# Routing's products over two slots and two banks, stores issued by ScalarE, and a later weight split, in a three-stage FFN kernel on one core

## The chip, the cores and the metric

The kernel runs on one core of a Trainium2 chip. The metric is the device time of that core in microseconds (us), the median of several executions. The engines are TensorE (PE; PEld is its weight load, which overlaps with the products), VectorE (DVE), ScalarE (ACT), GpSimd (POOL) and SyncE (SP), which in this kernel issues nearly all DMAs.

## The reference

Three computations follow each other, all in fp32, over 3072 tokens (4 batches of 768) of 256 numbers.

```python
# 1: attention with a decaying state, in chunks: x (4,8,768,32), a, B, C (state 16)
M = (C @ B^T) * L            # L: products of a, causal
y = M @ x + (C @ state) * decay_to_i ; state = decay_full * state + sum(B x decay_from_j)
# 2: FFN with a leaky unit, 256 -> 2048 -> 256
h = x @ w_in
g = np.maximum(h, 0.0) + alpha * np.minimum(h, 0.0)
x = g @ w_out
# 3: eight experts, one per token, 256 -> 1024 -> 256
logits = x @ w_gate + modality_bias[modality_id]
e_idx = np.argmax(logits, axis=1)
...
out[mask] = gate_w[mask, None] * (np.maximum(x[mask] @ w1[e], 0.0) @ w2[e])
```

## The kernel before

**Stages.** The tokens are 24 chunks of 128, in nine blocks of 2, 2, 2 and then six times 3 chunks (block 0 to 8). A block goes through attention, the first FFN, and routing. The routed rows are scattered to a table `srt` in DRAM, sorted by expert. At the end there are 14 *items*, each a page of 256 sorted rows with the weights of one expert. Every large fp32 product is made of three, from operands split in a high and a low part (xh, xl; wi_h, wi_l; gh, gl).

**Slots.** From block 3 on the order of all work is written out by hand: a list of slots, 16 for each of the six late blocks (one for each 128 of the 2048 inner columns) and 8 for each item. A slot holds six products that make `ph` of its own column, ACT's `t` and VectorE's `g` from it, the split of the slot before (ACT's `gh`, POOL's `gl`), and six products `px` of the column four slots earlier. `do(u, fn, ...)` puts one more step at the end of slot u. Each engine runs what it has strictly in that order. `at[k, c]` is the slot of block k, column c; `ui` is the first slot of the items.

**Routing.** Block k is routed in the slots of block k+1 (u is the first of them). For each chunk t of the block, `route_mm` makes the product `pxr` of the FFN's result with an identity and the gate's weights, and one slot later `route_act` has VectorE add the logits `L` and ACT copy the rows to `xr`. `route_b` finds the best expert, `route_exp` and `route_gate` its probability, `route_c` ranks the rows (the product `pr`), `route_d` scatters them.

**Banks.** PSUM has three buffers for `ph` (routing of blocks 0 to 2 takes from these), the banks x0, x1 and x2 (`px`, and in x2 one `pxr`, `pr` or, for items, `pt` at a time), and two buffers `s` (`ps`, the attention scores, which VectorE's `mt` reads; and an item's second `px3`).

**The split of B and C.** In the late blocks B and C come from a DRAM tile `bcs` of three bf16 parts. They are made in two groups: chunks 13 to 20 in columns 1 to 6 of block 3, chunks 21 to 23 in columns 1 to 6 of block 5. Each step (`split_part`) has ACT cast a part to a tile `part` (three buffers), VectorE subtract it from `rbc`, and a DMA store the part. `load_chunk` reads `bcs` again, on SP: one load of `ab` and five of `bs` for each chunk.

**The items' start.** `item_split(i, ...)` splits an item's weights, in eight steps, one a slot: an ACT cast and a VectorE subtraction. `tail_counts` casts the counts to `cnti` and issues eight stores on SP which clear the rows behind each expert's last one (`srt<-zr`); the loads of item 2's weights (`raw`) follow them on SP. `table_at` places five small steps that work out which expert a page has.

Of the kernel before, what the change touches and what calls it, by code (L numbers as in the profile page):

```python
# [8 lines left out]
F32 = mybir.dt.float32  # L9
# [10 lines left out]
P = 128  # L20
NB, NH, SEQ, HD, DS = 4, 8, 768, 32, 16
# [91 lines left out]
def ssm_moe_moe_kernel(  # L113
# [21 lines left out]
    nc = tc.nc  # L135
# [13 lines left out]
    ps_s = ctx.enter_context(tc.tile_pool(name="ps_s", bufs=2, space=PS))  # L149


    def mm(o, l, r, start, stop):
        nc.tensor.matmul(o, l, r, start=start, stop=stop)  # L153
# [4 lines left out]
    def vsub(o, x, y):  # L158
        nc.vector.tensor_tensor(o, x, y, ALU.subtract)  # L159
# [8 lines left out]
    bcs = dram.tile([2, NCH, 3, DS, NH * P], BF16, name="bcs")  # L168
# [190 lines left out]
    m2p = []  # L359
# [104 lines left out]
                tc.declare_no_dep(d.ins, o, reason="rows are disjoint")  # L464
            tails.append(d.ins)

    def route_ps(k, shape, nm):
        if k < NS:
            return ps_h.tile(shape, F32, tag="h", name=nm)
        return ps_x.tile(shape, F32, tag="x2", name=nm)  # L470

    def route_a(k, ts=None):

        n = blocks[k][1]
        for t in range(n) if ts is None else ts:
            route_mm(k, t)
            route_act(k, t)

    def route_mm(k, t):
        if t == 0:  # L480
            blk[k]["xr"] = work.tile([P, MX, ROW], F32, tag="xr", name="xr", bufs=2)
            blk[k]["L"] = small.tile([P, MX, NE], F32, tag="L", name="L")
        p = route_ps(k, [P, 512], "pxr")
        ts_ = slice(t * P, (t + 1) * P)
        pk = p[:, :KD * (P + NE)].rearrange("p (k w) -> p k w", k=KD)
        for kk in range(KD):
            mm(pk[:, kk], blk[k]["xT"][:, kk, ts_], idwg[:, kk], True, True)
        blk[k]["pk"] = pk
# [45 lines left out]
    def route_c(k):  # L534
        c0, n = blocks[k]
        oh = blk[k]["oh"]
        pr = route_ps(k, [P, 5, NE], "pr")
        for t in range(n + 1):
            for u in range(t):
                mm(pr[:, t], one, oh[:, u], u == 0, t == n and u == n - 1)  # L540
            if t < n:
                mm(pr[:, t], tri, oh[:, t], t == 0, True)
        blk[k]["pr"] = pr
# [405 lines left out]
    last = len(blocks) - 1  # L949
    slots = [("m",) + q for q in late] + [("i", i, fc) for i in range(NSTATIC) for fc in range(KF2)]  # L950
    at = {q[1:]: u for u, q in reversed(list(enumerate(slots))) if q[0] == "m"}
    ui = len(late)
# [3 lines left out]
    def do(u, fn, *args):  # L956
        todo.setdefault(u, []).append((fn, args))
# [42 lines left out]
    def split_part(g, j, q):  # L1000
        c0 = NEXACT + g * 8
        n = min(8, NCH - c0)
        r = blk["r", g, j]
        t = parts[-1].tile([P, NH * P], BF16, tag="part", name="part", bufs=3)
        nc.scalar.copy(t[:n * DS], r[:n * DS])
        if q < 2:
            vsub(r[:n * DS], r[:n * DS], t[:n * DS])
        nc.sync.dma_start(bcs[j, c0:c0 + n, q], t[:n * DS])

    def tail_counts():  # L1010
        nc.vector.tensor_copy(cnti, cnt)
# [11 lines left out]
    def route_at(k, mms, b):  # L1023
        for t, u in enumerate(mms):
            do(u, route_mm, k, t)
            do(u + 1, route_act, k, t)
        for v, fn in zip(b, (route_b, route_exp, route_gate, route_c, route_d)):
            do(v, fn, k)

    u = at[NS, 0]  # L1030
    route_at(1, (u, u + 1), (u + 4, u + 5, u + 6, u + 5, u + 6))
    route_at(2, (u + 5, u + 6), (u + 9, u + 10, u + 11, u + 10, u + 14))
    for k in range(NS, last + 1):
        u = at[k, 15] + 1
        if k < last - 1:
            route_at(k, (u + 4, u + 5, u + 6), (u + 8, u + 9, u + 12, u + 10, u + 13))
        else:
            route_at(k, (u + 4, u + 5, u + 6), (u + 7, u + 8, u + 9, u + 8, u + 9))

    def table_at(u, j, pool):  # L1040
        steps = []

        def step():
            if not steps:
                steps.append(item_tables(j, pool[-1]))
            next(steps[0], None)

        for v in range(u, u + 5):
            do(v, step)

    table_at(at[last - 1, 14], 0, small_)
    table_at(at[last, 10], 1, m2p)
    do(at[last, 15], tail_counts)
    table_at(ui + 11, 2, m2p)

    for k in range(NS, last):
        c0, n = blocks[k + 1]
# [3 lines left out]
        for j in range(n):  # L1061
            c, b = c0 + j, at[k, 0] + 5 * j - (k > NS)
# [11 lines left out]
    for g, u, v in ((1, None, at[NS, 1]), (2, at[NS + 1, 8], at[NS + 2, 1])):  # L1074
        if u is not None:
            do(u, split_load, g)
        for q in range(6):
            do(v + q, split_part, g, q % 2, q // 2)
# [10 lines left out]
    do(ui + 3, item_tr_act, 1)  # L1089
    for q in range(8):  # L1090
        do(at[last, 6] + q, item_split, 0, q // 2, (q % 2,))
        do(at[last, 11] + q, item_split, 1, q // 2, (q % 2,))
    for i in range(2, NSTATIC):
        b = ui + KF2 * (i - 2)
        do(b, item_load, i, 1 if i >= NFULL else 2)
        do(b if i == 2 else b + 5, item_rows, i)
        b += KF2
        for q in range(8):
            do(b + q, item_split, i, q // 2, (q % 2,))
        do(b + 4, item_tr_mm, i)  # L1100
        do(b + 5, item_tr_act, i)
# [102 lines left out]
```

## Time and profile before

| | |
|---|---|
| median of 3 runs | 628.76 us (627.92 to 630.45) |
| profiled execution, its own time | 629.47 us |
| its span | 627.7 us |
| mean granted TensorE clock | 0.938 |
| PE busy | 559.2 us |
| DVE busy | 438.0 us |
| ACT busy | 318.6 us |
| POOL busy | 242.0 us |
| DMA | 92.15 MB, mean 147 GB/s |

The span reaches from the first to the last instruction of the profiled execution; some 1.8 us of its time lie outside. A matmul's busy time contains its overlap with the next one. The granted clock is a share of full speed: 1.00 is 2.4 GHz, 0.50 is 1.2 GHz.

### The profile page before, as it was taken

Reading aid. Unit: us, or ns where it says so; the run is one execution under the profiler, and the core shown is the slowest. Engines: PE = TensorE matmul, PEld = TensorE weight load, DVE = VectorE, ACT = ScalarE, POOL = GpSimd, SP = SyncE. Lnnn points to the kernel's source line nnn. Section 1 sums busy time; section 2 is a strip of 40 time slices with the busy share of each in tenths; the row PEclk is TensorE's granted clock in tenths of the full one; section 3 lists DMA queues with packets and bytes.
Section 4 is the critical chain, followed back from the end, with each engine's and each line's share of the span. In section 5 each row is a group of like instructions: output and inputs, shape, how many; then the busy total and the mean of one; then the engine's idle time right before and its main releaser. Section 6 shows DMA issues by size and latency. Waiting matters only on the chain. (4 is left out here: it accounts for less than half of the span.)

```text
span 627.7 us, 12104 instructions
## 1 busy us (share of the span) xinstructions
PE 559.2 (89%) x4271; PEld 522.6 (83%) x4271; DVE 438.0 (70%) x861; ACT 318.6 (51%) x702; POOL 242.0 (39%) x258
## 2 busy tenths in 40 slices
PE   8988778998969989949989989988778999999994
PEld 7866667898869878938979979978778999999994
DVE  4997879935857756846766757549729787787770
ACT  0463655655634443624444434455526776776761
POOL 1142444654534635824654834635203121122211
PEclk9786797999869999979999999999898999999998
DMA  7967664310234325214214210270597977677500
GB/s 236 296 216 240 196 185 158 129 45 9 82 92 151 119 76 162 86 55 130 101 69 131 93 68 2 85 243 26 162 280 256 353 221 233 221 227 228 178 24 7
DMA packets 60563, 92.15 MB, mean 147 GB/s; under 512 B 5102, under 2 KB 37040, under 8 KB 60496
## 3 DMA queue, kind: packets, MB, share of 16 engines
q1 hardware_dynamic: 58096, 84.99, 43.0%
q0 software_dynamic: 2400, 6.32, 2.7%
q8 instruction: 36, 0.59, 0.4%
q14 instruction: 31, 0.25, 0.1%
HBM read 75.59 MB, written 15.96 MB: 146 GB/s over the span
## 5 line engine op out<-in xcount | busy, mean ns | idle before, releaser
L616 POOL TENSOR_TENSOR gl<-g,gh 128x384 fp32r<-128x384 f32 (+1 forms) x144 | 145.5, 1014 | 170.7 <-ACT gh L614 168.2
L607 DVE SCALAR_TENSOR_TENSOR g<-ph,sal,t 128x384 f32<-128x384 f32 (+1 forms) x144 | 81.0, 565 | 91.5 <-ACT t L605 91.4
L605 ACT ACTIVATE t<-ph,sgn 128x384 f32<-128x384 f32 (+1 forms) x144 | 78.4, 545 | 129.7 <-PE ph L153 128.4
L153 PE MATMUL ph<-xh,wi_h 128*128 128x384 f32 (+1 forms) x288 | 100.9, 351 | 12.9 <-DVE g L607 12.7
L153 PE MATMUL px<-gh,wo_h 128*128 128x384 f32 (+1 forms) x288 | 95.7, 333 | 2.4 <-ACT wo_h L424 1.4
L153 PE MATMUL px<-gl,wo_h 128*128 128x384 f32 (+1 forms) x288 | 96.1, 334 | 1.5 <-POOL gl L616 1.5
L153 PE MATMUL px<-gh,wo_l 128*128 128x384 f32 (+1 forms) x288 | 95.0, 331 | 0.0
L153 PE MATMUL ph<-xl,wi_h 128*128 128x384 f32 (+1 forms) x288 | 94.3, 328 | 0.3 <-DVE xl L159 0.3
L153 PE MATMUL ph<-xh,wi_l 128*128 128x384 f32 (+1 forms) x288 | 94.2, 327 | 0.0
L614 ACT CAST gh<-g 128x384 fp32r<-128x384 f32 (+1 forms) x144 | 67.5, 469 | 20.9 <-DVE g L607 20.6
L875 POOL DMA_INDIRECT out_dram<-ob,xr x26 | 28.4, 1092 | 111.9 <-ACT ob L874 26.4
L153 PEld LDWEIGHTS ph<-xh,wi_h 128*128 128x128 f32 x288 | 56.7, 198 | 17.6 <-DVE g L607 14.5
L852 ACT ACTIVATE rh<-ph 128x256 fp32r<-128x256 f32 (+1 forms) x112 | 41.5, 371 | 55.4 <-PE ph L153 55.1
L853 DVE SCALAR_TENSOR_TENSOR rl<-ph,rh 128x256 fp32r<-128x256 f32 (+1 forms) x112 | 45.0, 402 | 27.0 <-ACT rh L852 26.0
L153 PEld LDWEIGHTS px<-gh,wo_h 128*128 128x128 f32 x288 | 57.8, 201 | 2.8 <-ACT wo_h L424 1.6
L153 PEld LDWEIGHTS px<-gl,wo_h 128*128 128x128 f32 x288 | 57.4, 199 | 3.2 <-POOL gl L616 2.2
L153 PEld LDWEIGHTS px<-gh,wo_l 128*128 128x128 f32 x288 | 57.7, 201 | 0.2 <-issue 0.2
L153 PEld LDWEIGHTS ph<-xl,wi_h 128*128 128x128 f32 x288 | 56.8, 197 | 0.8 <-DVE xl L159 0.8
L153 PEld LDWEIGHTS ph<-xh,wi_l 128*128 128x128 f32 x288 | 56.7, 197 | 0.0
L153 PE MATMUL ph<-x2h,wi_h 128*128 128x256 f32 x144 | 41.6, 289 | 2.8 <-DVE rl L853 2.8
L962 DVE TENSOR_TENSOR_SCAN ab<-ab,id 128x512 f32<-128x512 f32 x30 | 43.6, 1453 | 0.0
L567 POOL DMA_INDIRECT srt<-xr,pi x24 | 25.5, 1062 | 43.4 <-DMA raw<-in_w_dram 29.9
(149 smaller groups left out, 1312.7 us busy)
## 6 DMA issues: line engine op xcount, KB each, us to landing
raw<-in_w_dram SPq DMA_DIRECT2D x56, 512.0 KB
ab<-a_scr SPq DMA_DIRECT2D x24, 512.0 KB
srt<-zr SPq DMA_DIRECT2D x8, 645.0 KB
raw<-in_w_in_dram SPq DMA_DIRECT2D x8, 512.0 KB
raw<-in_w_out_dram SPq DMA_DIRECT2D x8, 512.0 KB
bs<-bcs SPq DMA_DIRECT2D x38, 96.0 KB
bs<-bcs SPq DMA_DIRECT2D x19, 192.0 KB
xr<-srt SPq DMA_DIRECT2D x14, 258.0 KB
```

The lines of the kernel that those rows point to most:

```text
L153: nc.tensor.matmul(o, l, r, start=start, stop=stop)
L567: sc = nc.gpsimd.indirect_dma_start(out=srt[:, :], out_offset=bass.IndirectOffsetOnAxis(ap=pi[:, t:t + 1].bitcast(U32), axis=0), in_=xr[:, ...
L605: nc.scalar.activation(t[:, :N], ph[:, :N], AF.Copy, scale=sg)
L607: nc.vector.scalar_tensor_tensor(g[:, :N], ph[:, :N], sal[:, fc:fc + 1], t[:, :N], ALU.mult, ALU.max)
L614: nc.scalar.copy(gh[:, :N], g[:, :N])
L616: nc.gpsimd.tensor_tensor(gl[:, :N], g[:, :N], f(gh[:, :N]), ALU.subtract)
L852: nc.scalar.activation(rh[:, :n], ph[:, :n], AF.Relu)
L853: nc.vector.scalar_tensor_tensor(rl[:, :n], ph[:, :n], 0.0, f(rh[:, :n]), ALU.max, ALU.subtract)
L875: nc.gpsimd.indirect_dma_start(out=out[:, :], out_offset=bass.IndirectOffsetOnAxis(ap=xr[:, t, ROW - 1:ROW].bitcast(U32), axis=0), in_=ob, ...
L962: nc.vector.tensor_tensor_scan(lt[:, s_].rearrange("p h i -> p (h i)"), lt[:, s_].rearrange("p h i -> p (h i)"), id8[:, s_].rearrange("p h ...
```

## The change

There are three edits.

First, the routing of blocks 3 to 8: the second chunk's product moves from one slot behind the first to two, the third's to three, and the third takes a buffer of `s` and no longer bank x2. Steps b to d of blocks 1, 2, 7 and 8 are put in other slots to suit; those of blocks 3 to 6 stay.

Second, the twelve stores in `split_part` are issued by ACT and not by SP.

Third, the split of item 1's weights starts four slots later, so that half of it lies in item 0's slots; the item tables, `tail_counts` and the loads of later items' rows move by one slot. Lines of the changed kernel are two higher from `route_ps` on.

```diff
-    def route_ps(k, shape, nm):
+    def route_ps(k, shape, nm, t=0):
         if k < NS:
             return ps_h.tile(shape, F32, tag="h", name=nm)
+        if t == 2:
+            return ps_s.tile(shape, F32, tag="s", name=nm)
         return ps_x.tile(shape, F32, tag="x2", name=nm)
...
-        p = route_ps(k, [P, 512], "pxr")
+        p = route_ps(k, [P, 512], "pxr", t)
...
-        nc.sync.dma_start(bcs[j, c0:c0 + n, q], t[:n * DS])
+        nc.scalar.dma_start(bcs[j, c0:c0 + n, q], t[:n * DS])
...
     u = at[NS, 0]
-    route_at(1, (u, u + 1), (u + 4, u + 5, u + 6, u + 5, u + 6))
-    route_at(2, (u + 5, u + 6), (u + 9, u + 10, u + 11, u + 10, u + 14))
+    route_at(1, (u, u + 1), (u + 4, u + 5, u + 6, u + 6, u + 8))
+    route_at(2, (u + 5, u + 7), (u + 9, u + 10, u + 11, u + 11, u + 14))
     for k in range(NS, last + 1):
         u = at[k, 15] + 1
         if k < last - 1:
-            route_at(k, (u + 4, u + 5, u + 6), (u + 8, u + 9, u + 12, u + 10, u + 13))
+            route_at(k, (u + 4, u + 6, u + 7), (u + 8, u + 9, u + 12, u + 10, u + 13))
         else:
-            route_at(k, (u + 4, u + 5, u + 6), (u + 7, u + 8, u + 9, u + 8, u + 9))
+            route_at(k, (u + 4, u + 6, u + 7), (u + 8, u + 9, u + 10, u + 10, u + 10))
...
-    table_at(at[last, 10], 1, m2p)
-    do(at[last, 15], tail_counts)
-    table_at(ui + 11, 2, m2p)
+    table_at(at[last, 11], 1, m2p)
+    do(ui, tail_counts)
+    table_at(ui + 12, 2, m2p)
...
-        do(at[last, 11] + q, item_split, 1, q // 2, (q % 2,))
+        do(at[last, 15] + q, item_split, 1, q // 2, (q % 2,))
...
-        do(b if i == 2 else b + 5, item_rows, i)
+        do(b if i == 2 else b + 6, item_rows, i)
```

**PE, a middle block's route.** In block 4's slots PE's rows from the first `pxr` of block 3 on read as follows before (the second `pxr` is the last row; between the two stand the scores `ps` and one slot's twelve products, of which four rows are shown).

```order
L153 MATMUL pxr<-idwg,xT 128x136 x2
...
L153 MATMUL ps<-bs 128x128
L153 MATMUL ph<-xh,wi_h 128x384
...
L153 MATMUL px<-gh,wo_l 128x384
L153 MATMUL px<-gl,wo_h 128x384
L153 MATMUL pxr<-idwg,xT 128x136 x2
```

After the change the row that follows those twelve products is the weight load of the next scores:

```order
L153 MATMUL px<-gh,wo_h 128x384
L153 MATMUL px<-gh,wo_l 128x384
L153 MATMUL px<-gl,wo_h 128x384
L153 LDWEIGHTS bs
L153 MATMUL ps<-bs 128x128
```

The second `pxr` has moved behind the next slot's twelve products, the third behind one slot more.

**ACT, columns 4 to 6 of block 5.** Here stand the last casts of the second group (48 partitions are three chunks) and the copies `xr` of block 4's route. Before:

```order
L325 CAST xh<-py 128x2x128
L1005 CAST part<-rbc 48x1024
L605 ACTIVATE t<-ph,sgn 128x384
L614 CAST gh<-g 128x384
L497 COPY xr<-pxr 128x256
L1005 CAST part<-rbc 48x1024
L605 ACTIVATE t<-ph,sgn 128x384
L614 CAST gh<-g 128x384
L497 COPY xr<-pxr 128x256
```

After:

```order
L325 CAST xh<-py 128x2x128
L1007 CAST part<-rbc 48x1024
L1010 DMA bcs<-part 3x16x1024
L607 ACTIVATE t<-ph,sgn 128x384
L616 CAST gh<-g 128x384
L499 COPY xr<-pxr 128x256
L1007 CAST part<-rbc 48x1024
L1010 DMA bcs<-part 3x16x1024
L607 ACTIVATE t<-ph,sgn 128x384
L616 CAST gh<-g 128x384
```

Each store now stands in ACT's own order directly behind its cast, in front of the slot's `t`; the second copy `xr` is a slot later.

**VectorE, the end of block 8.** `x2l` is the low part of item 0's rows, `rl` that of the first item's inner values, `wi_l` and `wo_l` are here the low parts of item 1's weights. Before:

```order
L836 TENSOR_TENSOR x2l<-pt,x2h 128x512
L159 TENSOR_TENSOR wi_l<-raw_5072,wi_h 128x2x256
L607 SCALAR_TENSOR_TENSOR g<-ph,sal,t 128x384
L1011 CAST cnti<-cnt 128x8
L159 TENSOR_TENSOR wo_l<-raw_5074,wo_h 128x512
L853 SCALAR_TENSOR_TENSOR rl<-ph_5512,rh 128x256
```

After:

```order
L838 TENSOR_TENSOR x2l<-pt,x2h 128x512
L609 SCALAR_TENSOR_TENSOR g<-ph,sal,t 128x384
L159 TENSOR_TENSOR wi_l<-raw_5070,wi_h 128x2x256
L855 SCALAR_TENSOR_TENSOR rl<-ph_5423,rh 128x256
L1013 CAST cnti<-cnt 128x8
L159 TENSOR_TENSOR wi_l<-raw_5070,wi_h 128x2x256
```

`cnti` has moved from before the first `rl` to behind it, and the subtractions here belong to an earlier part of item 1's weights.

## Rows read from the trace of the kernel before

**Rows 1.** The page's part 1: busy time, share, instructions.

```profile
PE 559.2 (89%) x4271; PEld 522.6 (83%) x4271; DVE 438.0 (70%) x861; ACT 318.6 (51%) x702; POOL 242.0 (39%) x258
```

**Rows 2.** Waits of PE: us in total, times, longest us.

```profile
PE pxr L153 <- ACT xr L497: 20.8, 12, 9.0
```

**Rows 3.** PE's timeline, block 3's route: start, us, operation [idle before <-releaser].

```profile
222.27 0.42 PE L153 MATMUL ph<-xh,wi_h 128*128 128x384 f32 x1
...
225.90 0.73 PE L153 MATMUL pxr<-idwg,xT 128*128 128x136 f32 x4 [1.29 <-ACT xr L497]
...
226.66 0.42 PE L153 MATMUL ph<-xh,wi_h 128*128 128x384 f32 x1
...
230.07 0.73 PE L153 MATMUL pxr<-idwg,xT 128*128 128x136 f32 x4 [1.09 <-ACT xr L497]
...
230.56 0.42 PE L153 MATMUL ph<-xh,wi_h 128*128 128x384 f32 x1
...
232.72 0.34 PE L153 MATMUL ph<-xh,wi_h 128*128 128x384 f32 x1
```

**Rows 4.** PE's timeline, block 4's route in block 5's slots 5 to 8.

```profile
267.68 0.42 PE L153 MATMUL ph<-xh,wi_h 128*128 128x384 f32 x1
...
279.07 1.27 PE L153 MATMUL pxr<-idwg,xT 128*128 128x136 f32 x4 [9.02 <-ACT xr L497]
...
287.57 0.33 PE L153 MATMUL ph<-xh,wi_h 128*128 128x384 f32 x1
```

**Rows 5.** ACT's timeline, the first and fourth cast of the second group.

```profile
258.96 1.05 ACT L1005 CAST part<-rbc 48x1024 bf16<-48x1024 f32 x1
...
275.51 1.04 ACT L1005 CAST part<-rbc 48x1024 bf16<-48x1024 f32 x1 [6.56 <-DMA bcs<-part]
```

**Rows 6.** SP's timeline of DMA issues there: start, us, xcount issues.

```profile
262.36 2.13 SPq L192 DMA_DIRECT2D bs<-bcs  x3
...
266.25 14.39 SPq L1008 DMA_DIRECT2D bcs<-part  x5
```

**Rows 7.** The view of tile part: ns of one issue, min/median/max; first and last start.

```profile
L1008 SPq DMA_DIRECT2D bcs<-part x12: 572/640/707, 162.8 to 289.7; - x12
```

**Rows 8.** Windows: PE, PEld, DVE, ACT, POOL busy (instructions), granted clock, DMA share, GB/s.

```profile
184.00:186.00 2.00, 2.00 (x7) 2.00 (x7) 1.27 (x2) 1.31 (x2) 1.85 (x1) 0.50 0.09 35
274.00:276.00 2.00, 0.00 (x0) 0.00 (x0) 0.00 (x0) 0.49 (x1) 0.00 (x0) 0.50 0.13 50
```

**Rows 9.** PE's timeline, block 3's slots 6 to 9.

```profile
174.14 0.45 PE L153 MATMUL ph<-xh,wi_h 128*128 128x384 f32 x1 [0.61 <-DVE g L607]
...
182.18 1.28 PE L153 MATMUL pxr<-idwg,xT 128*128 128x136 f32 x4 [4.13 <-DVE g L607]
...
189.97 0.34 PE L153 MATMUL ph<-xh,wi_h 128*128 128x384 f32 x1
```

**Rows 10.** ACT's timeline, a cast of the first group in block 3.

```profile
179.89 1.04 ACT L1005 CAST part<-rbc 128x1024 bf16<-128x1024 f32 x1 [5.14 <-DMA bcs<-part]
```

**Rows 11.** Windows, same columns: the last block's later slots.

```profile
420.00:440.00 20.00, 17.59 (x107) 16.41 (x105) 19.00 (x43) 12.56 (x27) 10.50 (x10) 1.00 0.06 21
```

**Rows 12.** DVE's timeline at the end of the last block.

```profile
442.78 0.67 DVE L836 TENSOR_TENSOR x2l<-pt,x2h 128x512 fp32r<-128x512 f32 x1
...
444.51 0.44 DVE L1011 CAST cnti<-cnt 128x8 int32<-128x8 f32 x1
...
445.47 0.41 DVE L853 SCALAR_TENSOR_TENSOR rl<-ph,rh 128x256 fp32r<-128x256 f32 x1
```

**Rows 13.** SP's timeline, the clears.

```profile
445.79 12.63 SPq L461 DMA_DIRECT2D srt<-zr  x8
```

**Rows 14.** ACT's timeline, the first cast of item 2's weights.

```profile
470.24 0.62 ACT L814 CAST wi_h<-raw 128x512 fp32r<-128x512 f32 x1 [6.16 <-DMA raw<-in_w_dram]
```

**Rows 15.** PE's timeline, the first slots of item 0 and of item 1.

```profile
443.51 0.39 PE L153 MATMUL ph<-x2l,w1h 128*128 128x256 f32 x1 [2.55 <-DVE x2l L836]
...
471.97 0.58 PE L153 MATMUL ph<-x2h,wi_h 128*128 128x256 f32 x1 [2.76 <-DVE rl L853]
```

## The prediction

> **What bounds the kernel now.** I read the busy shares first [rows 1]: TensorE (PE) works 89% of the span, ScalarE (ACT) 51%. A gain has to come out of PE's own gaps, and ACT can take more work unless it falls where ACT is already late. The waits of PE come next [rows 2]: the largest is of routing's product pxr for the copy xr on ACT, 20.8 us in 12 times, 9.0 in the longest. PE's timeline then shows two kinds of this wait. In the ordinary one [rows 3], pxr of the next chunk needs bank x2, which ACT has to copy out, and the copy stands in ACT's queue behind the previous slot's t and gh: 1.29 and 1.09 us in one route. The other is the 9.02 us at 279.07 [rows 4]. There ACT itself stood still: the fourth cast of the split of B and C had to wait 6.56 us for a store of part [rows 5], since there are three part buffers, and t, gh and the copy xr stand behind the cast. The store, ready when the cast of 258.96 ended at 260.01, went out on SP's queue at 266.25 only, behind a chunk's loads [rows 6]. Block 3, where the first group is split, shows the same shape: ACT 5.14 us in front of a cast [rows 10], PE 4.13 us in front of pxr [rows 9].
>
> **Routes of blocks 3, 5, 6, 7.** Block 3's route, in block 4's slots, is the pattern. From 222.27 to 230.56 are two slots, 8.29 us [rows 3]. A slot of twelve products alone takes 230.56 to 232.72 = 2.16; pxr with the score products behind it takes 0.76 (225.90 to 226.66) and 0.49 (230.07 to 230.56). The pair should take 2 x 2.16 + 0.76 + 0.49 = 5.57, so 2.72 is lost: 1.29 and 1.09 of waiting, and 0.34 of slower products right behind it. After the change the second pxr stands a slot later, when the copy is long done, and the third has another bank, whose last reader (VectorE's mt) is a slot old. I give both waits back: 4 x 2.72 = **10.9**. Blocks 5 to 7 show the same two waits in the trace. Bounds: 4 x 1.2 = 4.8 if one of the two stays, 10.9.
>
> **Block 4's route, with the second group of stores.** Slots 5 to 8 run from 267.68 to 287.57 [rows 4], 19.89. Without the stall the three slots are the 10.45 of 222.27 to 232.72 less the 2.72, so 7.73: 12.2 is lost. The store issued by ACT right behind its cast leaves at about 260.0 and not at 266.25, ahead of the loads, and the fourth cast finds its buffer free. In return each cast is followed by an issue of about 0.64 on ACT: that is what the 12 stores took on SP [rows 7], and the nearest row there is. Cast and issue together, 1.7 us, now stand in front of t in a slot of 2.16, so I leave 0.5 of a wait for xr: **11.6**. Bounds: 8 to 12.2.
>
> **Block 3, with the first group.** Slots 6 to 8 take 174.14 to 189.97 [rows 9], 15.83, and need 3 x 2.16 + 0.76 = 7.24: 8.6 is lost, 4.13 idle and the rest at a granted clock of 0.50. At that clock PE made 7 products in 2 us [rows 8], against 107 in 20 us at 1.00 [rows 11], so a third is lost. Not all of it returns. The routes of blocks 1 and 2 take buffers of ph, of which there are three; their products and ranks make ph of the next slots wait for the g of the slot just before, with cast and issue on ACT in front of t. By my walk through these slots the waits are 1.0, 2.0, 1.5 and 0.25, about 4.7 of the 8.6: **4.0** back. Bounds: 0 to 8.6.
>
> **ACT's stores elsewhere.** 12 x 0.64 = 7.7 us of ACT's time, covered by its idle half [rows 1] except in the slots above, where they are counted. Without that cover, the whole 7.7 is lost.
>
> **The item split and tail_counts.** In the last block VectorE is the bound: busy 19.00 us of 420 to 440 [rows 11]. Item 1's split starts four slots later, so three subtractions leave from in front of x2l, about 1.8 us by the 0.67 of the same shape. But cnti, 1.73 behind x2l today (442.78 to 444.51 [rows 12]), now stands behind item 0's first rl, which runs 0.96 after cnti today; I put it 2.6 behind x2l. So cnti comes 0.9 earlier against the block. From cnti runs a chain which the change doesn't shorten: eight clears on SP [rows 13], item 2's loads queued behind them, and the first cast of item 2's weights, at 470.24 after 6.16 of waiting for the load [rows 14]: 25.7 us from 444.51. PE waits for it 2.76 us [rows 15]. So whatever PE saves in these slots (the 2.55 in front of x2l [rows 15], block 8's pxr waits) comes back as a longer wait in item 1, some 8 to 9 us in all; only the 0.9 counts. A longer wait means a longer stretch at half clock behind it, some 2 us of which costs 0.7 by rows 8 and 11: **0.2** net. Bounds: -1.5 (cnti late by another subtraction and a longer clock recovery) to 3.
>
> **The other moves** (tables, item rows a slot later, steps b to d of the last two blocks) stay on idle VectorE and SP with slots to spare: 0.
>
> **Sum.** 10.9 + 11.6 + 4.0 + 0.2 = 26.7. The profiled execution took 629.47, 0.7 above the median of 628.76: 602.8 against its own time, 602.1 against the median. I say **602.0**.
>
> **Rival A: the store lands as late from ACT.** It was issued at 266.25 and the cast that needed its buffer ran at 275.51 [rows 5, 6]: 9.2 us for 48 x 2 KB. The DMA engines were at 0.13 then, 50 GB/s [rows 8]. At that rate 96 KB take 1.9 us, so I hold most of the 9.2 for the loads ahead of it. If the 9.2 is the store's own, casts follow each other by some 2.2 us, the fourth comes 6.6 after the first, and the first's store lands 10.3 after its cast began: 3.7 lost in one group or in both, 606 to 610, and 607 as its middle. The Trainium skill, "DMA: Bandwidth & Descriptors", section "Issuing engines are not separate DMA queues", speaks for this rival: DMAs of any engine run on the same 16 DMA engines and interleave, and issuing from several saves only the issuing sequencer's time. By that rule the change gains the issue's wait, 6.2 us of it, and no faster landing; the trace so far shows only the first half. Chance 0.12.
>
> **Rival B: the item slots gain too.** If cnti comes early enough and the loads behind the clears are quicker with less else in flight, PE's 2.76 and part of the new wait vanish: 6 to 9 us more, 593 to 596. Against it: the clears and loads took 25.7 us with nothing of the attention left to compete. Chance 0.06.
>
> **Rival C: ACT is held at some stores.** If a store has to wait for an earlier DMA to land, say two of six in each group for half of 9.2, ACT and the PE behind it lose some 18 us: 620. For it: ACT's queue has no slack in these slots. Chance 0.06.
>
> **Rival D, slower: ACT is held at every store until it has landed.** That would be 12 x (9.2 - 0.64) = 103 us: 602 + 103 = 705. It decides from 26.7 / 12 = 2.2 us of holding a store. Against it: SP issues three loads in 2.13 us [rows 6] and does not wait for them to land; but the five stores behind took 14.39 together, as each waits for its cast. Chance 0.04.
>
> **Rival E: the waits only change their name**, since the slots need ACT as much as before and the ph chain takes up what pxr gave: within 3 us of before. Chance 0.03.
>
> **The numbers.** The forecast has 0.69, A 0.12, B 0.06, C 0.06, D 0.04, E 0.03. The bounds of the terms, 4.8 to 10.9, 8 to 12.2, 0 to 8.6 and -1.5 to 3, add up to 11.3 and 34.7, which would be 617 and 594, but hardly all lie at one end. For 8 in 10 the range takes in A and the lower part of B: **594 to 612**. Half a per cent, 3 us, is about what can be told from no change: faster 0.93, same 0.03, slower 0.04.
>
> **What would show it.** Right: no wait of ACT's cast for bcs, pxr's 20.8 us down to one or two, twelve stores on ACT's queue at 0.6 to 0.7, the clock no longer at 0.50 around 274, ph of block 3's slots 7 to 9 waiting for g by one or two us each, and a wait of 8 to 9 us in front of item 1's products with ACT waiting for raw. Wrong: ACT idle in front of a part cast or a store (A, C, D), no such wait in item 1 (B), or waits of ph for g in every slot that has a route (E).

## The result, and the profile after

The changed kernel takes 600.88 us (600.14 to 603.31, 4 runs) against 628.34 for the kernel before on the same chip: a ratio of 0.9564, 95% interval 0.9529 to 0.9599. The forecast was 602.0. The profiled execution took 600.14 with a span of 598.3, at a mean granted clock of 0.950.

The page's part 1 of the changed kernel answers to [rows 1]: the same 4271 products take 10 us less of PE's time, at a higher mean clock, and the span is 29 us shorter.

```profile
PE 549.2 (92%) x4271; PEld 515.5 (86%) x4271; DVE 437.9 (73%) x861; ACT 319.0 (53%) x702; POOL 242.0 (40%) x258
```

PE's waits (total, times, longest) answer to [rows 2]. The 20.8 us of pxr for xr are down to one wait of 0.8 and another of 0.8 for mt; what leads now is ph waiting for g, and one wait in the items.

```profile
PE ph L153 <- DVE g L609: 14.4, 9, 5.5
PE ph L153 <- DVE rl L855: 5.6, 1, 5.6
PE ph L153 <- DVE x2l L838: 2.5, 1, 2.5
...
PE pxr L153 <- DVE mt L978: 0.8, 1, 0.8
PE pxr L153 <- ACT xr L499: 0.8, 1, 0.8
```

PE's timeline of block 3's route, the place of [rows 3]: no row of pxr has a wait behind it, and slots 5 to 8 take 216.02 to 223.49, 7.47 us, where they took 10.45.

```profile
215.36 0.63 PE L153 MATMUL pxr<-idwg,xT 128*128 128x136 f32 x4
216.02 0.42 PE L153 MATMUL ph<-xh,wi_h 128*128 128x384 f32 x1
...
220.57 0.62 PE L153 MATMUL pxr<-idwg,xT 128*128 128x136 f32 x4
...
223.11 0.62 PE L153 MATMUL pxr<-idwg,xT 128*128 128x136 f32 x4
223.49 0.42 PE L153 MATMUL ph<-xh,wi_h 128*128 128x384 f32 x1
```

Block 4's route, the place of [rows 4]: slots 5 to 8 are 258.63 to 268.27, 9.64 for 19.89, with two waits of 0.80 left.

```profile
258.63 0.42 PE L153 MATMUL ph<-xh,wi_h 128*128 128x384 f32 x1
...
264.17 0.73 PE L153 MATMUL pxr<-idwg,xT 128*128 128x136 f32 x4 [0.80 <-ACT xr L499]
...
267.79 0.73 PE L153 MATMUL pxr<-idwg,xT 128*128 128x136 f32 x4 [0.80 <-DVE mt L978]
268.27 0.42 PE L153 MATMUL ph<-xh,wi_h 128*128 128x384 f32 x1
```

ACT's timeline there answers to [rows 5, 6]: the first store leaves right behind its cast, and the fourth cast has no wait in front. The last row, from the view of tile part, is the issue's price on ACT: 0.68, where SP took 0.64 [rows 7].

```profile
249.91 1.04 ACT L1007 CAST part<-rbc 48x1024 bf16<-48x1024 f32 x1
250.98 0.77 ACTq L1010 DMA_DIRECT2D bcs<-part  x1
...
259.80 1.04 ACT L1007 CAST part<-rbc 48x1024 bf16<-48x1024 f32 x1
260.88 0.68 ACTq L1010 DMA_DIRECT2D bcs<-part  x1
...
L1010 ACTq DMA_DIRECT2D bcs<-part x12: 583/682/1179, 160.1 to 267.8; - x12
```

Where the time came from, and what the experiments did, is read best from the length of each stretch. The table's numbers are differences between starts in VectorE's timelines: of g of the first column of blocks 3 to 8, of the cast of cnti, and of rl of item 1's second column (the first work that stands behind item 2's weights). From there to the last rl all kernels take 145 to 147. Blocks 3 to 7 are 24.5 of the 29.3 us between the two profiled executions, block 8 up to cnti 3.7, in the places that the prediction named, but for 2.2 us of block 3 that the rows below the table explain.

| us | block 3 | block 4 | block 5 | blocks 6, 7 | block 8 to cnti | cnti to item 1 |
|---|---|---|---|---|---|---|
| before | 57.23 | 45.53 | 54.40 | 88.31 | 44.06 | 26.99 |
| changed | 51.46 | 42.75 | 44.22 | 82.54 | 40.40 | 26.75 |
| e1 stores alone | 49.58 | 45.72 | 48.01 | 88.37 | 44.10 | 28.26 |
| e2 routes alone | 54.51 | 42.74 | 50.20 | 82.54 | 40.86 | 27.99 |
| e3 items alone | 53.78 | 45.72 | 53.75 | 88.23 | 43.96 | 27.85 |
| e5 more buffers | 47.58 | 45.62 | 46.56 | 88.31 | 44.09 | 27.88 |
| e6 one bank | 51.41 | 44.19 | 48.41 | 85.19 | 41.77 | 28.56 |
| e7 early clears | 51.39 | 42.74 | 44.25 | 82.55 | 27.62 | 31.88 |
| e8 halved stores | 55.94 | 42.76 | 49.18 | 82.54 | 40.12 | 29.14 |
| e9 buffers, early clears | 51.03 | 42.85 | 43.05 | 82.54 | 27.62 | 32.12 |
| e10 old tables | 49.65 | 42.86 | 44.25 | 82.55 | 39.91 | 27.79 |
| e11 combined | 49.58 | 42.87 | 43.00 | 82.56 | 27.63 | 31.59 |

These 2.2 us are not the change's. In the kernel before, block 3's first step, from g of its first column to g of its second, took 5.52 us; it took 3.29 to 3.31 in the eleven other kernels, e3 among them, whose code there is that of the kernel before. Only in that one of the twelve profiled executions was the granted clock low there, 0.52 from 154 to 161 us; why is not known. The rows are of the kernel before and of the changed one (PE, PEld, DVE, ACT, POOL busy, clock, DMA share, GB/s):

```profile
154.00:161.00 7.00, 6.48 (x29) 6.11 (x28) 3.17 (x5) 2.21 (x5) 2.94 (x4) 0.52 0.11 38
154.00:161.00 7.00, 6.42 (x48) 6.02 (x47) 5.58 (x9) 3.35 (x7) 4.49 (x4) 1.00 0.11 38
```

The columns of the blocks repeat to 0.2 where the code is the same, except block 3 of the kernel before without its first step (51.71, and 50.47 in e3), its block 5 (54.40, and 53.75 in e3), and block 8 to cnti of the changed kernel (40.40, 40.12 in e8, 39.91 in e10); the last column does not repeat. Block 3 began between 154.51 and 158.41, latest in e3, e5, e8 and e9.

### The profile page after: what moved, and what is told of

Read it like the earlier page. It is cut to its first block, busy times and chain, and to the rows that moved or that the text cites. A ratio compares the mean times of both kernels' runs of the same rounds, so it can differ in the third digit from the quotient of the medians.

```text
span 598.3 us, 12098 instructions
## 1 busy us (share of the span) xinstructions
PE 549.2 (92%) x4271; PEld 515.5 (86%) x4271; DVE 437.9 (73%) x861; ACT 319.0 (53%) x702; POOL 242.0 (40%) x258
## 5 line engine op out<-in xcount | busy, mean ns | idle before, releaser
L153 PE MATMUL px<-gl,wo_h 128*128 128x384 f32 (+1 forms) x288 | 94.9, 330 | 1.7 <-POOL gl L618 1.7
L153 PE MATMUL ph<-xl,wi_h 128*128 128x384 f32 (+1 forms) x288 | 93.1, 324 | 0.3 <-DVE xl L159 0.3
L153 PE MATMUL ph<-xh,wi_l 128*128 128x384 f32 (+1 forms) x288 | 93.0, 323 | 0.0
L153 PEld LDWEIGHTS px<-gh,wo_l 128*128 128x128 f32 x288 | 56.5, 197 | 0.2 <-DVE wo_l L159 0.2
```

## The experiments

**e1: only the stores.**

```diff
-        nc.sync.dma_start(bcs[j, c0:c0 + n, q], t[:n * DS])
+        nc.scalar.dma_start(bcs[j, c0:c0 + n, q], t[:n * DS])
```

> Only the twelve stores of part go to ACT; routes and items as before. Theory (a store waits on SP behind a chunk's loads, and the cast that needs its buffer holds up t, gh and xr): block 3's slots give back some 5 us and block 4's route 8 to 10, while the ordinary pxr waits (four routes, 2.9 each in the changed kernel) stay: 628.3 - 14 = 614, range 611 to 617, no wait of a part cast for bcs, pxr's waits still above 12 us. Rival 1 (the routes' spacing gives all, the stores nothing): 626 to 629. Rival 2 (the stores alone take ACT's time from the routes, which stand close together): ACT's issues of 0.68 in front of t cost in each split slot, 620 to 625.

618.08 (616.64 to 619.49), ratio 0.9816 (0.9762 to 0.987), just above the range expected. By the table blocks 3 and 5 give 7.65 and 6.39, the 14 expected, but 2.2 of the first number is the low clock of the kernel before. So the stores gave 5.4 in block 3, as expected, and 6.4 in block 5, where 8 to 10 was expected. Their sum, 11.8, agrees with the 12.2 by which the whole lies below the kernel before in the same comparison (630.29). pxr's waits are 15.0 us in 12 times. Rival 1 with nothing from the stores is out, and so is rival 2, which left them 3 to 8.

**e2: only the routes.** The diff is the first edit, route_ps with the four calls of route_at.

> Only the routes' products are spaced and the third has its own bank; stores on SP, items as before. Theory: 2.9 for each of the routes of blocks 3, 5, 6 and 7 comes back, 11.6, and little of block 4's, where ACT still stands still for a store: 628.3 - 12.5 = 616, range 613 to 618, ACT still waiting 10 us or more for bcs in front of part casts. Rival (the wider spacing also covers ACT's stall, so that the stores are not needed): 600 to 606. Block 8's own waits give nothing at the end, since the item start follows cnti.

613.09 (611.29 to 615.65), ratio 0.9733 (0.9672 to 0.9793). Blocks 4, 6 and 7 are as short as in the changed kernel, 2.8 to 2.9 each, and block 8 up to cnti 3.2. Block 5 gives 4.2 where the whole change gives 10.2, and block 3, without its first step, 0.5. ACT's timeline shows the store's wait untouched, 6.41 us, so the spacing doesn't cover it and the rival is out:

```profile
270.48 1.04 ACT L1007 CAST part<-rbc 48x1024 bf16<-48x1024 f32 x1 [6.41 <-DMA bcs<-part]
```

**e3: only the items.**

```diff
-    table_at(at[last, 10], 1, m2p)
-    do(at[last, 15], tail_counts)
+    table_at(at[last, 11], 1, m2p)
+    do(ui, tail_counts)
...
-        do(at[last, 11] + q, item_split, 1, q // 2, (q % 2,))
+        do(at[last, 15] + q, item_split, 1, q // 2, (q % 2,))
```

> Only the split of item 1 four slots later, the tables, tail_counts and the rows' loads a slot later. Theory (the end follows cnti by 25.5 us of clears and loads): cnti moves by less than 1 us against block 8, so 627.5, range 626.5 to 629, with the wait in front of item 1's fifth unit at 3 to 7 us. Rival (relieving VectorE in the last slots shortens the end itself): 623 to 625.

The other two numbers of the third edit, for the last table and the items' rows, are moved with it.

628.3 (626.48 to 631.8), ratio 0.9978 (0.9947 to 1.0009): no difference that can be told. Block 8 up to cnti is 0.1 shorter. The wait in front of x2l is 2.5, as before, and the one in item 1 is 4.3. The three profiled executions' gains of e1, e2 and e3, 12.8, 16.3 and 0.8 against 629.47, add up to 29.9, and the whole change gave 29.3. This says less than it seems, since the 2.2 us of the low clock are in each of the four numbers. By the medians the three are 12.2, 17.2 and 2.0 below 630.29, together 31.4, and the whole change gave 27.5 in its own comparison. So the edits do touch each other: in block 3 e1 and e2 give 5.4 and 0.5 alone, and the whole change 3.6.

**e5: the stores left on SP, more buffers.** This tells who issues from what the cast waits for.

```diff
-                t = pool.tile([P, NH * P], BF16, tag=tag, name="part", bufs=3)
+                t = pool.tile([P, NH * P], BF16, tag=tag, name="part", bufs=4)
...
-        t = parts[-1].tile([P, NH * P], BF16, tag="part", name="part", bufs=3)
+        t = parts[-1].tile([P, NH * P], BF16, tag="part", name="part", bufs=4 if len(parts) == 1 else 6)
```

> The kernel before with stores still on SP, but four part buffers in the pool of the first groups and six in that of the last group, so that the second group's six casts never wait for a store. Theory (the cost was the cast's wait for its buffer, not who issues): block 4's route gains 9 to 11 and block 3's some 3 to 6: 615, range 612 to 618. Rival (a store that goes out late also makes the chunk's later loads late, and these then hold the slots): 622 to 628, with a new wait of the scores for bs.

617.11 (616.37 to 618.13), ratio 0.9792 (0.9738 to 0.9846), as much as e1. Block 5 gives 7.84, more than e1's 6.39 and less than the 9 to 11 expected; block 3 is 2.0 shorter than in e1. The fourth cast follows in its slot without a wait:

```profile
252.56 1.04 ACT L1005 CAST part<-rbc 48x1024 bf16<-48x1024 f32 x1
...
258.72 1.05 ACT L1005 CAST part<-rbc 48x1024 bf16<-48x1024 f32 x1
...
262.44 1.04 ACT L1005 CAST part<-rbc 48x1024 bf16<-48x1024 f32 x1
```

On SP the stores of the second group go out from 259.95 on, 6.4 us after the first cast's end at 253.60:

```profile
259.95 8.13 SPq L1008 DMA_DIRECT2D bcs<-part  x5
```

So the cost was the cast's wait for a buffer, whose store stood late in SP's queue. That ACT issues the store is one cure; a store that goes out late does no harm if nobody needs its buffer.

**e6: the third product back in bank x2.**

```diff
-        if t == 2:
-            return ps_s.tile(shape, F32, tag="s", name=nm)
```

> The changed kernel with the third product back in bank x2, in its new slot. Theory (the second product needs the two slots, the third needs the bank, since the copy of the second stands right in front of it in ACT's queue): one wait of 1.0 to 1.3 us in each of the routes of blocks 3 to 7 returns, with slower products behind it some 6.5 in all, and block 8's is hidden by the wait for item 2's weights: 607.5, range 605.5 to 609. Rival (two slots between first and second are what counts, the bank nothing): 600 to 602.

613.15 (612.16 to 614.29), ratio 0.9738 (0.9708 to 0.9768), 4 us above the range expected. In blocks 4, 6 and 7 and in block 8 1.3 to 1.4 us each come back as a wait of the third product, as the first row below; 5.5 in all. In block 5 it is 4.2: there the second copy stands behind casts and stores on ACT, and the third product waits 3.53.

```profile
225.71 0.73 PE L153 MATMUL pxr<-idwg,xT 128*128 128x136 f32 x4 [1.10 <-ACT xr L497]
...
273.23 1.27 PE L153 MATMUL pxr<-idwg,xT 128*128 128x136 f32 x4 [3.53 <-ACT xr L497]
```

The rest, some 3 us, lies outside the routes: block 3 began 1.3 later in this execution and the stretch behind cnti took 28.56. Both parts of the edit are needed, the bank for half of the ordinary gain.

**e7: the clears five slots earlier.**

```diff
-    do(ui, tail_counts)
+    do(at[last, 11], tail_counts)
```

> The changed kernel with the cast of cnti and the eight clears five slots earlier, in the last block's twelfth slot, where the counts of blocks 0 to 7 are already final; the same work. Theory (PE's wait of 5.64 in item 1 ends when item 2's weights land, 25.5 us after cnti, because they queue behind the clears): the wait goes, and with it the low clock behind it, 4 to 5 us: 596.5, range 595 to 598. Rival (the wait moves to the next thing, the rows of item 1 or 2 or the last block's scatter, or the clears slow the last block): 599.5 to 601.5.

594.0 (590.93 to 596.63), ratio 0.9439 (0.939 to 0.9488), a microsecond below the range expected, and faster than the changed kernel by more than the 5.64 that PE waited. The wait of ph for rl is gone from PE's waits. cnti and item 1's second column together take 59.50 for the changed kernel's 67.15, 7.65 less. Beside the wait the low clock behind it is gone: the mean granted clock was 0.57 from 439 to 447 us in the changed kernel, and is 1.00 from 420 to 460 in e7. On SP the loads of item 2's weights now begin at 419.66, where in the changed kernel (second fence) they begin at 430.33; in both they start about a microsecond after the last clear is out.

```profile
404.44 14.38 SPq L461 DMA_DIRECT2D srt<-zr  x8
419.66 8.18 SPq L784 DMA_DIRECT2D raw<-in_w_dram  x4
```

```profile
416.89 12.33 SPq L461 DMA_DIRECT2D srt<-zr  x8
430.33 5.20 SPq L784 DMA_DIRECT2D raw<-in_w_dram  x4
...
441.37 0.62 ACT L816 CAST wi_h<-raw 128x512 fp32r<-128x512 f32 x1 [7.55 <-DMA raw<-in_w_dram]
...
443.10 0.58 PE L153 MATMUL ph<-x2h,wi_h 128*128 128x256 f32 x1 [5.64 <-DVE rl L855]
```

**e8: each store as two of half the width.** The bytes are the same, and the number of issues on ACT doubles; each row that a store writes has 1 KB in place of 2.

```diff
-        nc.scalar.dma_start(bcs[j, c0:c0 + n, q], t[:n * DS])
+        w = NH * P // 2
+        for s in range(2):
+            nc.scalar.dma_start(bcs[j, c0:c0 + n, q, :, s * w:(s + 1) * w], t[:n * DS, s * w:(s + 1) * w])
```

> The changed kernel with each store of part issued by ACT as two of half the width, so that ACT issues 24 and not 12; the same bytes. Theory (in the split slots ACT is already the engine that PE waits for, so an issue costs what it takes, 0.68): 12 more cost most of 8.2 us: 607, range 604 to 609. Rival (ACT's idle half covers the issues also here): 600 to 602.

613.95 (611.02 to 617.55), ratio 0.9749 (0.9694 to 0.9803), above the range expected. Block 3 loses 4.5 and block 5 5.0 against the changed kernel, and no other block anything: 9.4 for twelve issues, 0.8 each, a little over the 0.68 that one takes. Some 2 of the 9.4 are waiting: two of the 24 issues stood still for 1.1 and 1.6 us, and one of the changed kernel's twelve for 0.7 (rival C below says for what). That leaves 0.6 for an issue. (The whole lost 13: the rest lies in a later start of block 3 and in the stretch behind cnti.) ACT's timeline shows the pair in front of t:

```profile
270.76 1.04 ACT L1007 CAST part<-rbc 48x1024 bf16<-48x1024 f32 x1
271.83 1.42 ACTq L1012 DMA_DIRECT2D bcs<-part  x2
273.30 0.58 ACT L607 ACTIVATE t<-ph,sgn 128x384 f32<-128x384 f32 x1 [1.49 <-PE ph L153]
```

In the split slots ACT's issues are therefore paid about in full, though the engine is idle for half of the span. What the shorter rows cost was not tried by itself.

**e9: early clears, and the stores back on SP with the buffers of e5.** The diff is that of e7 and e5, with nc.sync in place of nc.scalar.

> The version with early clears, and the stores of part back on SP with four buffers in the first groups' pool and six in the last group's. Theory (a cast without a wait for its buffer needs no store on ACT, and ACT saves its twelve issues): block 3's and block 5's split slots gain 1 to 4 us over the version with early clears: 594.5, range 592 to 596.5. Rival (with the routes closed up, the late stores make the loads of the last chunks late, and the slots wait for these): 598 to 603.

592.05 (590.05 to 595.09), ratio 0.9394 (0.9361 to 0.9427), which can't be told from e7 by the times. Block 5 is 1.2 shorter than in e7, block 3 only 0.4: four buffers leave a wait of 1.3 us of a cast for a store there. The gain expected is there mainly in one of the two places.

**e10: the route tables of blocks 1 and 2 as before.**

```diff
-    route_at(1, (u, u + 1), (u + 4, u + 5, u + 6, u + 6, u + 8))
-    route_at(2, (u + 5, u + 7), (u + 9, u + 10, u + 11, u + 11, u + 14))
+    route_at(1, (u, u + 1), (u + 4, u + 5, u + 6, u + 5, u + 6))
+    route_at(2, (u + 5, u + 6), (u + 9, u + 10, u + 11, u + 10, u + 14))
```

> The changed kernel with the route tables of blocks 1 and 2 as before. Theory (block 3's slots return 5.3 in the changed kernel and 7.2 with the stores alone, because the new tables of blocks 1 and 2 put the ph of three slots behind the g just made): 1.8 come back by block 3's fifth slot, and the whole is 599, range 597.5 to 600.5. Rival (the two closed-up slots then need ACT's cast and issue where they have the copy xr in front, and the gain is lost by block 4's start): no difference there, 600 to 602.

601.4 (600.0 to 602.45), ratio 0.9553 (0.9518 to 0.9588): above the range expected, and not faster. Block 3 is 1.8 shorter, as the theory has it, and the gain lasts to cnti (1.6 earlier). There it is lost: the stretch behind cnti takes 27.79 for 26.75, and PE's wait in item 1 grows from 5.64 to 7.26:

```profile
442.51 0.58 PE L153 MATMUL ph<-x2h,wi_h 128*128 128x256 f32 x1 [7.26 <-DVE rl L855]
```

**e11: together.** The diffs of e7 and e10, and for the second group only six buffers with nc.sync (the first group keeps ACT and three).

> The changed kernel with the clears five slots earlier, the route tables of blocks 1 and 2 as before, and the second group's stores back on SP with six buffers. Theory: 594.0 of the version with early clears, less 1.8 of block 3's slots, less 1.2 that block 5's split slots gained with six buffers: 591, range 589 to 593.5. Rival (these gains are of slots that wait for something else as well): 593.5 to 596.

591.81 (589.68 to 593.47, 6 runs), ratio 0.9399 (0.937 to 0.9427). The profiled execution's 589.68 is 10.5 below the changed kernel's, and the stretches add up: 1.9 in block 3, 1.2 in block 5, and 7.9 from block 8's first column to item 1, less 0.5 of a later start. It beats both kernels; by the times it can't be told from e9 or e7.

## Why the prediction was right, by its steps

Against the profiled execution's own time the sum was 26.7, and 29.3 was measured, 2.2 of it the low clock of the kernel before; between the medians it is 27.5. The mechanism of the two large terms was right. The four terms miss by 1.1, -1.4, -0.4 and 0.8, so that the sum came so close is in part luck.

**Routes of blocks 3, 5, 6, 7: 10.9 forecast, 12.0 measured** (2.8, 2.9, 2.9 in blocks 4, 6 and 7; for block 7's route 3.4, from g of block 8's fifth column to that of its ninth). Each slot pair lost both waits and the slower products behind them, by the mechanism given; e2 shows the gain from this edit alone, and e6 that the second bank carries half of it, which the prediction had only argued.

**Block 4's route: 11.6 forecast, 10.2 measured.** The mechanism is shown twice, by e1 (store earlier) and e5 (store as late, no buffer needed). The left-over wait was sized at 0.5; it is two of 0.80. The cause of the first is the one the prediction gave, cast and issue in front of t; e8 prices an issue there at 0.6 to 0.8. The second is the third product's wait for mt. The prediction held this reader of its bank to be a slot old, but in this route VectorE reaches it only just before the product of 267.79:

```profile
267.05 1.28 DVE L978 TENSOR_TENSOR mt<-ps,ab 128x512 f32<-128x512 f32 x2
```

The clock, at 0.50 around 274 in the kernel before [rows 8], stays at 1.00 from 250 to 268 in the changed one. Only three of the ten microseconds are the ordinary route's; e2 alone gives 4.2.

**Block 3: 4.0 forecast, 3.6 measured** (5.8 by the table, less the 2.2 of its first step). The columns from the sixth on gave 4.9. The four steps ahead of them lost 1.3: from g of the second column to g of the sixth is 14.28 for 12.98, by ACT's issues in front of t (14.25 in e1; 13.01 in e5, whose stores stay on SP). The prediction put ACT's stores outside the stalled slots at nothing, and here they were not covered. The part of the loss that stays was put at 4.7. The reason given for it, that blocks 1 and 2 take ph's buffers with their routes, holds: with the old tables e10 gives back 1.8 more, so the new tables of these blocks cost something. The walk made it too large: in PE's timeline of the changed kernel the waits of ph for g are 2.06, 0.17 and 0.34, against 1.0, 2.0, 1.5 and 0.25.

```profile
176.34 0.44 PE L153 MATMUL ph<-xh,wi_h 128*128 128x384 f32 x1 [2.06 <-DVE g L609]
...
180.90 0.44 PE L153 MATMUL ph<-xh,wi_h 128*128 128x384 f32 x1 [0.17 <-DVE g L609]
183.63 0.44 PE L153 MATMUL ph<-xh,wi_h 128*128 128x384 f32 x1 [0.34 <-DVE g L609]
```

**Item split and tail_counts: 0.2 forecast, 1.0 measured**, 0.2 of it ahead of cnti and 0.8 behind, where executions differ by more than that; alone (e3) nothing that the times can tell. That the end follows cnti held: e10's gain of 1.6 ahead of cnti did not reach the end, and e7, which moved cnti, gained more than any edit of the items. Inside the step two pieces were mis-sized. Against g of block 8's ninth column x2l came 1.5 earlier (19.09 us behind it for 20.59), not 1.8, and cnti stands 3.0 behind x2l, not 2.6, since the rl in front of it waits for ACT. So cnti gained 0.2, not 0.9. VectorE's rows answer to [rows 12]:

```profile
412.86 0.68 DVE L838 TENSOR_TENSOR x2l<-pt,x2h 128x512 fp32r<-128x512 f32 x1
...
415.54 0.42 DVE L855 SCALAR_TENSOR_TENSOR rl<-ph,rh 128x256 fp32r<-128x256 f32 x1 [0.88 <-ACT rh L854]
415.88 0.16 DVE L1013 CAST cnti<-cnt 128x8 int32<-128x8 f32 x1
```

The prediction also had PE's 2.55 in front of x2l come back in item 1. That wait stayed, at 2.5, and the wait of 8 to 9 us in item 1 came out as 5.64, shorter by about as much.

**The rivals.** A (the store lands as late from ACT) fell: no cast of the changed kernel waits for bcs, and the first store, out at 250.98, did not hold the fourth cast at 259.80. The trace has the packets by queue, and ACT's queue, q10, carries these twelve stores alone. All of the first store's packets are through 3.5 us after its issue; the row is of the window from 250.9 to 254.5 (packets, MB, share of the 16 DMA engines):

```profile
q10 hardware_dynamic: 51, 0.10, 9.2%
```

With the packets counted off in the order of the stores, the other eleven took 3.7 to 7.9 us from issue to last packet, against 9.2 from SP. The price of this rival was wrong as well: the first and the fourth cast stand 9.9 us apart, not 6.6, so that 9.2 would have held the fourth by 0.4. The Trainium skill, "DMA: Bandwidth & Descriptors", section "Issuing engines are not separate DMA queues", says that issuing from several engines only saves the issuing sequencer's time. Here that time was not small: it was the place behind a chunk's loads, 6.2 us, and with it two stalls; e5, where issue and landing stay as they were, agrees that the landing was not what had to become faster. D fell with e8: an issue costs 0.6 to 0.8 on ACT, not a landing. C came true in small: one store of the twelve, the fourth in block 3, was issued 0.77 behind the end of its cast, where 0.03 is usual.

```profile
168.95 1.05 ACT L1007 CAST part<-rbc 128x1024 bf16<-128x1024 f32 x1
170.77 0.59 ACTq L1010 DMA_DIRECT2D bcs<-part  x1
```

By the trace's semaphore events this issue waited for a semaphore on which it and SP's load of `ab` (issued at 164.66) both count, and the load's last count came at 170.70. e1, e10 and e11 show the same wait, and in e8 two issues waited for such a load, until 172.39 and 264.00. B came true only when the clears were moved (e7), and E fell with the size of the gain.

**What stays open.** The stretch behind cnti took 26.75 to 29.14 in the nine traces in which PE waits for it, with the same clears and loads; why was not tried. The changed kernel's trace has the shortest of them, so a microsecond of its 29.3 may be luck of that execution, beside the 2.2 of the low clock in the trace of the kernel before.

## What to carry to other kernels

Where an engine waits for a buffer, look at who still holds it and in which queue that work stands: a store that is ready but stands behind loads on the same queue costs as much as a slow one, and either another issuer or more buffers cures it, the second without taking time from a busy engine. An engine's idle half doesn't pay for an issue in slots where that engine is on the path; double the issue to see its price. Where two queues count on one semaphore, an issue can also wait for the other queue's load. Before the difference of two profiled executions is put down to a change, compare the stretches in which the code is the same: here 2.2 us of 29.3 lay in one. Before relieving the last slots of a stage, find the chain that starts the next one: what was saved ahead of cnti became a longer wait behind it, and moving cnti itself by five slots gave 7 us.

## What the runs showed of the hardware that was not expected

A VectorE step of the table, a product of two tiles of 128x288, took 3.70 us in the kernel before and 3.71 in the changed one, and 0.44 in e3, where instead the scan ahead of it took 4.26 in place of 0.76. In each case the long one ran while GpSimd had three subtractions gl to do in a row, held up by the scatters ahead of them. The rows are VectorE's of the kernel before and of e3, with GpSimd's of the same time:

```profile
428.61 0.76 DVE L714 TENSOR_TENSOR_SCAN rk<-cst,sets 128x288 f32<-128x288 f32 x1
430.39 3.70 DVE L723 TENSOR_TENSOR rk<-rk,sets 128x288 f32<-128x288 f32 x1
...
430.82 2.94 POOL L616 TENSOR_TENSOR gl<-g,gh 128x384 fp32r<-128x384 f32 x3
```

```profile
428.23 4.26 DVE L714 TENSOR_TENSOR_SCAN rk<-cst,sets 128x288 f32<-128x288 f32 x1
433.52 0.44 DVE L723 TENSOR_TENSOR rk<-rk,sets 128x288 f32<-128x288 f32 x1
...
428.91 2.96 POOL L616 TENSOR_TENSOR gl<-g,gh 128x384 fp32r<-128x384 f32 x3
```

The long step ends 0.3 us after GpSimd's run in the first fence, 0.6 in the second. The Trainium skill, "GPSIMD Engine Reference", section "1. Specifications", says that GpSimd's SBUF interfaces are shared with VectorE and that there is contention with VectorE instructions that have two SBUF inputs; both long steps have two, and the rows agree, 3.3 and 3.5 us being lost each time. No experiment took GpSimd's run away, so the cause is argued, not shown.
